# Sorting one batch's v in natural layout through DRAM, and a 96-column stationary operand for late scores, in a fused block-sort attention and feed-forward kernel

## The chip, the cores and the metric

The kernel runs on one core of a Trainium2 chip. The metric is device microseconds of one execution, the median of several. Most executions of the kernel before agree within 0.3%.

## The reference

Four batches of eight heads, 768 tokens, 64 values per head. A small matrix per head, made doubly stochastic by five rounds of normalisation (Sinkhorn), mixes ("sorts") the 8 blocks of 96 tokens of k and v. Each block of q then attends to its own sorted block, and the result goes through a feed-forward layer with a squared ReLU.

```python
k_sorted = np.einsum('bhij,bhjcd->bhicd', P, k_b)      # P: 8 x 8 per head, blocks of 96 tokens
v_sorted = np.einsum('bhij,bhjcd->bhicd', P, v_b)
scores = scale * np.matmul(q_b, k_sb.transpose(0, 1, 2, 4, 3))
attn = np.exp(scores - max); attn = attn / attn.sum()
x = np.matmul(attn, v_sb)                              # then (3072, 512) tokens
out = np.maximum(x @ w_in, 0.0) ** 2 @ w_out           # d_ff = 2048
```

## The kernel before

In a matmul call `lhsT` is the stationary operand, which a weight load puts into the array, and `rhs` is the moving one. A small planner orders all instructions ahead of time, so that attention work of the next batch stands between the feed-forward matmuls of the one before. Batches are numbered from 0 in the code and from one in the text. Heads are worked on in pairs (`hp`), in two groups (`g`) of two pairs.

The first two batches sort k and v with a product that transposes at the same time; v has to be turned back for the attention-value product:

```python
def s_sort(u, t, ...):                 # t: 1 = k, 2 = v
    for a in range(NA):                # 6
        for h in range(2):
            nc.tensor.matmul(out=tp[64 * h:64 * (h + 1), a, :],
                lhsT=src[:, 2 * u.hp + h, D * a:D * (a + 1)],          # 64 columns
                rhs=w_all[:, H * u.b + 2 * u.hp + h, ...])
def s_vt(u, ...):                      # 8 transposes of 128 x 128 turn v back
    nc.tensor.transpose(out=vbp[:, n, :], in_=u.vsT[:, i // NQ, ...], identity=ident)
```

The last two batches sort in natural layout with the array cut into 32x32 tiles. v is then written to DRAM and read back in another partition order, k is turned by a DMA transpose into `kx`. In `kx` the 8 blocks are interleaved, so one block's stationary operand is every eighth element:

```python
def s_nat(b, g, t, due):               # 16 matmuls of 32 x 32 weights, 384 columns
    ...
    nc.sync.dma_start(out=v_way[b, g]..., in_=vn_r[m]...)   # write
    nc.sync.dma_start(out=vb_r[w]..., in_=v_way[b, g]...)   # read back
def s_sc(u, ...):
    nc.tensor.matmul(out=scp[:, h, BLK * n:BLK * (n + 1)],
        lhsT=(u.ksT[64 * h:64 * (h + 1), hf, BLK * n:BLK * n + 128] if u.b < 2 else
              kx_r[u.kx][64 * h:64 * (h + 1), NQ * hf + n::NB]),    # 128 columns, step NB = 8
        rhs=...)                                                     # 96 columns
```

`kx` is 1024 elements wide, of which 256 are zeros, so that the operand has 128 columns although a block has only 96 tokens. Loads go through GpSimd's software DMA queue in a fixed order; two buffers each of q, k and v alternate between the batches.

The softmax here doesn't subtract the row's maximum and nothing guards it: scores larger than these inputs give would overflow.

Of the kernel before, what the change touches and what calls it, by code (L numbers as in the profile page):

```python
# [128 lines left out]
def kernel(  # L129
# [103 lines left out]
    for n in range(3):  # L233
        vb_r.append(const.tile([96, NB, HP, 66], BF16, name=f"vblk{n}"))
    v_way = nc.dram_tensor("v_way", (B, 2, NA, 128, HP * 66), BF16, kind="Internal").ap()

    kn_r = [const.tile([128, NA, 2, D], BF16, name=f"kn{n}") for n in range(3)]
    qi_r = [const.tile([128, NA, 2, D], BF16, name=f"qi{n}") for n in range(2)]
    kx_r = []
    for n in range(3):  # L240
        kx = const.tile([128, 128 * NB], BF16, name=f"kx{n}")
        nc.vector.memset(kx[:, 128 * NA:], 0.0)
        kx_r.append(kx)
    for n in range(4):
        et = const.tile([96, 2, HS + 32], BF16, name=f"et{n}")
        nc.vector.memset(et[:, :, HS:HS + 32], 0.0)
# [5 lines left out]
    xT = const.tile([128, KC, n_tok], BF16)  # L252
    w_all = const.tile([128, NH // 2, NB, C0], BF16)
    w_t = const.tile([128, NH // 4, 4, NB], BF16)
    qkv = {}
    landed = {}

# [14 lines left out]
    def load(b, t, h0, n, p=slice(0, 128)):  # L272
        def dst_src():
            alloc_qkv(b)
            if b > 1 and t:
                return (qkv[b][t].rearrange("p (g h) x -> p g (h x)", h=HP)[:, h0 // HP, :],
                        kv_t[t][b, :, h0 // HP, :])
            return qkv[b][t][p, h0:h0 + n, :], (q_r, k_r, v_r)[t][b, p, h0:h0 + n, :]
        dma((b, t, h0, p.start), 1.57 * n / H * (p.stop - p.start) / 128, dst_src,
            readers[b - 2] + [x_done[b - 1, x, 0] for x in range(HP)] if b > 1 else [])  # L280
# [26 lines left out]
    load_w_in(0)  # L307
    for g in range(1, 4):
        load_w_in(g)
    for g in range(4):  # L310
        t = slice(NT // 4 * g, NT // 4 * (g + 1))
        dma(("w_out", g), 1.05, lambda t=t: (w_out_bf[:, t, :], w_out_r[:, t, :]))
    for g in range(2):
        for t in (2, 1, 0):
            load(1, t, HP * g, HP)


    rs = const.tile([NH, NB], FP32)
# [83 lines left out]
    def build_wt(due):  # L402

        st = {}
        pick = const.tile([128, NB, 4], BF16, name="pick")
        picked = plan.add("DVE", 0.2, lambda e: nc.vector.tensor_copy(
            out=pick, in_=ident.rearrange("p (j c) -> p j c", c=C0)[:, :, 0:4]), [x_done[0, HP - 1, 0]])

        def mm(e):
            st["p"] = ps1.tile([128, NB, NH // 4], FP32, tag="p1", name="wtp")  # L410
            for h in range(4):
                nc.tensor.matmul(
                    out=st["p"][32 * h:32 * (h + 1), :, :].rearrange("p i g -> p (i g)"),
                    lhsT=pick.rearrange("p j c -> p (j c)"),
                    rhs=pt.rearrange("p i (g h) -> p h i g", h=4)[:, h, :, :],
                    start=True, stop=True)

        def fn(e):
            nc.vector.tensor_tensor(
                out=w_t,  # L420
                in0=mask_t[:, None, :, None].to_broadcast([128, NH // 4, 4, NB]),
                in1=st["p"].rearrange("p i g -> p g i")[:, :, None, :]
                .to_broadcast([128, NH // 4, 4, NB]),
                op=ALU.mult)

        s1, old = r1.take()
        pe = plan.add("PE", 0.15, mm, [cp, picked] + old, due, mode="col32")
        built["t"] = plan.add("DVE", 0.45, fn, [pe])
        r1.use(s1, pe, built["t"])


    class Unit:
# [101 lines left out]
    def s_sc(u, due=0):  # L534
# [3 lines left out]
        for hf in u.halves:  # L538
# [4 lines left out]
            def mm(e, hf=hf, st=st, slot=slot):  # L543
                qT = tiles["qT", u.b, u.hp]
                if u.b < 2:
                    qT = qT.rearrange("p a x -> p (a x)").rearrange("p (i q) -> p i q", q=BLK)
                st["p"] = scp = p2[slot]
                for n in range(NQ):
                    for h in range(2):
                        nc.tensor.matmul(  # L550
                            out=scp[:, h, BLK * n:BLK * (n + 1)],
                            lhsT=(u.ksT[64 * h:64 * (h + 1), hf, BLK * n:BLK * n + 128]
                                  if u.b < 2 else
                                  kx_r[u.kx][64 * h:64 * (h + 1), NQ * hf + n::NB]),
                            rhs=(qT[64 * h:64 * (h + 1), NQ * hf + n, :] if u.b < 2 else
                                 qT[64 * h:64 * (h + 1), :, C0 * (NQ * hf + n):
                                    C0 * (NQ * hf + n + 1)]),
                            start=True, stop=True)

            s2 = slot  # L560
            u.et[hf], olde = ret.take()
            pe = plan.add("PE", 0.17 if u.b < 2 else 0.26, mm, [u.k_op, u.q_op] + old, due,
                          mode="row")
            r2.use(s2, pe)
            rqT.use(qTs[u.b, u.hp], pe)
# [51 lines left out]
    def s_nat(b, g, t, due):  # L617
# [4 lines left out]
        for hp in (2 * g, 2 * g + 1):  # L622
            slot, old = r2.take()
            if t == 1:
                m, oldm = rkn.take()

            def mm(e, hp=hp, slot=slot):
                src = qkv[b][t].rearrange("p (g h) x -> p g (h x)", h=HP)
                for h in range(2):
                    r = slice(32 * (2 * (hp % 2) + h), 32 * (2 * (hp % 2) + h + 1))  # L630
                    for c in range(4):
                        nc.tensor.matmul(  # L632
                            out=p2[slot][32 * c:32 * (c + 1), h, 0:NA * D],
                            lhsT=w_t[r, HP // 2 * b + g, :, :].rearrange("p c i -> p (c i)"),
                            rhs=src[r, g, NA * D * c:NA * D * (c + 1)],
                            start=True, stop=True, tile_position=(r.start, 32 * c))

            def ev(e, hp=hp, slot=slot, m=m):
                dst = (vn_r[m][:, :, 2 * (hp % 2):2 * (hp % 2) + 2, 0:D] if t == 2
                       else kn_r[m])  # L640
                copy(e, dst, p2[slot][:, :, 0:NA * D].rearrange("p e (a d) -> p a e d", d=D))

            pe = plan.add("PE", 0.15, mm, [landed[b, t, HP * g, 0], built["t"]] + old, due,
                          mode="tile")
            readers[b].append(pe)
            op = plan.add(AD, cost_f(2 * NA * D), ev, [pe] + oldm)
            r2.use(slot, pe, op)
            evs.append(op)
            if t == 1:
                rkn.use(m, op)  # L650
                k_nat[b, hp] = m, op
# [1 line left out]
            return  # L653

        def write(e):
            nc.sync.dma_start(out=v_way[b, g].rearrange("a p x -> p a x"),
                              in_=vn_r[m].rearrange("p a h x -> p a (h x)"))

        w, oldw = rvb.take()

        def read(e):
            nc.sync.dma_start(
                out=vb_r[w].rearrange("p i h x -> p (i h x)"),
                in_=v_way[b, g].rearrange("a (c i) x -> (a c) (i x)", i=NB))

        wr = plan.add("SP", 0.33, write, evs + [loaded(b)])
        there = plan.add("WAY", 2.0, lambda e: None, [wr])
        rd = plan.add("SP", 0.33, read, [there] + oldw)
        back = plan.add("WAY", 2.0, lambda e: None, [rd])
        rvn.use(m, *evs, there)  # L670
        rvb.use(w, back)
        v_blk[b, g] = w, back
# [4 lines left out]
    def s_turn(b, hp):  # L677
# [3 lines left out]

        def k_turn(e):
            nc.sync.dma_start_transpose(
                out=kx_r[kx][:, 0:128 * NA].rearrange("p (a x) -> p a x", a=NA),
                in_=kn_r[m].rearrange("p a e d -> p (a e d)"))

        sp = plan.add("SP", 1.25, k_turn, [op, loaded(b)] + oldx)
# [26 lines left out]

    def s_av(u, due=0):
        nao, olda = rao.take()
        if u.b > 1:
            w, u.vs_op = v_blk[u.b, u.hp // 2]
        u.norms = []
        for hf in u.halves:  # L720
# [4 lines left out]
            def mm(e, hf=hf, st=st, slot=slot):  # L725
# [3 lines left out]
                for n in range(NQ):  # L729
                    for h in range(2):  # L730
                        nc.tensor.matmul(  # L731
                            out=oup[:, h, 66 * n:66 * n + D + 1],
                            lhsT=et_r[u.et[hf]][:, h, BLK * n:BLK * n + 128],
                            rhs=(u.vs[:, NQ * hf + n, h, 0:D + 1] if u.b < 2 else
                                 vb_r[w][:, NQ * hf + n, 2 * (u.hp % 2) + h, 0:D + 1]),
                            start=True, stop=True)

# [13 lines left out]
            op = plan.add("DVE", 0.9, norm, [pe])  # L751
            r2.use(s2, pe, op)
            ret.use(u.et[hf], pe)
            if u.b < 2:
                rks.use(u.n, pe)
            else:
                rvb.use(w, pe)
# [179 lines left out]
    def lay(b, halves, c0, c1):  # L937
        step, gap = (c1 - c0) / (HP + 0.9), (c1 - c0 - 13) / (HP - 1)
        for hp in range(HP):
# [3 lines left out]
            def open_(due, b=b, hp=hp, box=box):  # L943
# [2 lines left out]
                if b == 1:  # L946
                    build_w(H * b + 2 * hp, 2, pt, kops[b - 1, hp])
                u.k_op = kops[b, hp] = s_sort(u, 1, due)
                u.v_op = s_sort(u, 2, due)

            for f, s in ((0.0, open_),
                         (0.35, lambda due, box=box: s_sc(box["u"], due)),
                         (0.5, lambda due, box=box: s_vt(box["u"], due)),
                         (0.75, lambda due, box=box: s_av(box["u"], due)),
                         (1.2, lambda due, box=box: s_xt(box["u"], due))):
                todo.append((c + step * f, len(todo), s, b))
# [1 line left out]
    def lay_late(b, c0):  # L958

        todo.append((c0, len(todo), lambda due: load_late(b), 0))  # L960
        if b == 2:
            todo.append((c0, len(todo), build_wt, 0))
        for g in range(2):
            for t in (1, 2):
                todo.append((c0 + 9 + 9 * g, len(todo),
# [17 lines left out]
                load(b, t, HP * g, HP)  # L983

    lay(0, (1,), 0, n_up)
    lay(1, (0, 1), n_up, 2 * n_up)
    lay_late(2, 2 * n_up)
    lay_late(3, 4 * n_up)
# [45 lines left out]
```

## Time and profile before

| | before |
|---|---|
| median | 226.36 us (226.29 to 226.46, 4 runs) |
| span of the profiled run | 224.3 us |
| TensorE busy | 216.6 us, 97% |
| granted clock | 1.00 |

TensorE bounds the kernel; the prediction below shows the page's lines.

### The profile page before, as it was taken

How to read it: one execution, taken by the hardware profiler on the slowest of the kernel's cores; microseconds unless marked ns; L12 is line 12 of the kernel's file. 1: busy time of each engine (PE TensorE's matmuls, PEld its weight loads, DVE VectorE, ACT ScalarE, POOL GpSimd, SP SyncE). 2: the span in 40 equal slices, each digit the busy share in tenths (PEclk: the TensorE clock that was granted, in tenths of full speed). 3: DMA queues.
4: the chain of work that ended last, by engine and by line, in shares of the span. 5: the costliest groups of instructions: out<-in, count | busy, mean ns of one | idle time of the engine just before them, and what ended most of it. 6: DMA issues, size and time to landing. Idle time of an engine off the chain costs nothing.

```text
span 224.3 us, 5245 instructions
## 1 busy us (share of the span) xinstructions
PE 216.6 (97%) x2130; PEld 122.9 (55%) x2145; DVE 105.7 (47%) x297; ACT 122.1 (54%) x253; POOL 26.4 (12%) x46
## 2 busy tenths in 40 slices
PE   7898999999999999999999999999999999999994
PEld 2476665556665645545665455445665465446553
DVE  6777777317666416640666127523664045005400
ACT  4665776228885328734775248535774177137521
POOL 7962332200004200000000000000000000000000
PEclk9999999999999999999999999999999999999999
DMA  5999999999953996499941320899522410110012
GB/s 66 201 202 208 207 206 205 203 227 245 210 65 27 191 239 145 115 216 201 220 38 35 85 94 0 164 225 254 110 37 43 122 47 1 50 57 37 0 50 94
DMA packets 42744, 28.83 MB, mean 129 GB/s; under 512 B 22752, under 2 KB 38368, under 8 KB 42720
## 3 DMA queue, kind: packets, MB, share of 16 engines
q0 software_dynamic: 13888, 13.63, 37.1%
q1 hardware_dynamic: 28832, 14.86, 29.7%
q8 instruction: 17, 0.28, 0.5%
q14 instruction: 7, 0.06, 0.1%
HBM read 28.89 MB, written 7.91 MB: 164 GB/s over the span
## 4 chain that ended last, share of the span: by engine, by line
PE 92%; DMA 2%; DVE 2%; ACT 1%; issue 1%; ACTq 0%; POOLq 0%
PE hp L810 37%; PE op L838 35%; PE p L550 4%; PE p L731 3%; DMA qb<-in_q_dram 2%; PE p L510 2%; PE qtp L461 2%; PE vbp L598 2%; PE op L872 2%; PE p L350 1%; PE p L632 1%; PE xtp L779 1%; PE tp L510 1%; DVE ao L742 1%; ACT h L818 0%
## 5 line engine op out<-in xcount | busy, mean ns | idle before, releaser
L810 PE MATMUL hp<-xT,w_in_bf 128*128 128x384 bf16 x512 | 91.0, 326 | 0.0
L838 PE MATMUL op<-w_out_bf,h 128*128 128x512 bf16 x353 | 82.6, 379 | 0.8
L818 ACT ACTIVATE h<-hp 128x384 bf16<-128x384 f32 x128 | 62.0, 495 | 23.5 <-PE hp L810 20.0
L821 DVE TENSOR_TENSOR h<-h 128x384 bf16<-128x384 bf16 x128 | 44.5, 355 | 56.3 <-ACT h L818 55.5
L810 PEld LDWEIGHTS <-w_in_bf 128*128 128x128 bf16 x512 | 47.0, 98 | 30.0 <-issue 0.7
L838 PEld LDWEIGHTS <-h 128*128 128x128 bf16 x368 | 34.7, 98 | 39.4 <-issue 0.7
L192 ACT COPY ob<-op 128x512 f32<-128x512 f32 (+1 forms) x25 | 14.2, 569 | 56.0 <-PE op L838 50.6
L742 DVE TENSOR_TENSOR ao<-p,rec 96x512 bf16<-96x512 f32 x32 | 22.0, 687 | 1.4 <-DVE rec L741 0.3
L582 ACT ACTIVATE et<-p 96x384 bf16<-96x384 f32 x48 | 19.4, 491 | 2.4 <-PE p L550 2.4
L741 DVE RECIPROCAL rec<-p 96x8 f32<-96x8 f32 x32 | 6.4, 199 | 13.6 <-PE p L731 13.3
L731 PEld LDWEIGHTS <-et 96*128 96x128 bf16 x256 | 10.6, 97 | 2.9
L261 POOL DMA_DIRECT2D qb<-in_q_dram x8 | 6.0, 754 | 32.5 <-PE qtp L461 24.4
L350 PE MATMUL p<-ones 128*128 128x512 bf16 (+1 forms) x36 | 8.8, 360 | 1.1 <-DVE ones L213 1.1
L194 DVE COPY vs<-vbp 96x512 bf16<-96x512 bf16 (+1 forms) x12 | 6.1, 508 | 7.1 <-PE vbp L598 6.9
L573 ACT ACTIVATE et<-p 96x768 bf16<-96x768 f32 x8 | 6.3, 802 | 2.1 <-PE p L550 2.0
L261 POOL DMA_DIRECT2D kb<-in_k_dram x10 | 6.6, 659 | 6.6 <-DMA w_in_bf<-in_moe_w_in_dram 2.2
L261 POOL DMA_DIRECT2D vb<-in_v_dram x10 | 6.6, 660 | 6.4 <-DMA w_in_bf<-in_moe_w_in_dram 3.6
L192 ACT CAST ksT<-p 128x768 bf16<-128x768 f32 (+1 forms) x7 | 4.6, 662 | 3.3 <-PE p L510 3.3
L550 PEld LDWEIGHTS <-kx 64*128 64x128 bf16 x128 | 4.6, 155 | 2.8 <-issue 2.8
L731 PE MATMUL p<-vs,et 96*128 96x65 bf16 x128 | 6.0, 193 | 0.0
L461 PE MATMUL qtp<-ident,qb 64*64 64x64 bf16 (+1 forms) x144 | 4.7, 204 | 1.3 <-DMA qb<-in_q_dram 1.3
L461 PEld LDWEIGHTS <-qb 64*64 64x64 bf16 (+1 forms) x144 | 3.5, 109 | 4.5 <-DMA qb<-in_q_dram 2.3
(78 smaller groups left out, 129.3 us busy)
## 6 DMA issues: line engine op xcount, KB each, us to landing
out_dram<-ob SPq DMA_DIRECT2D x23, 256.0 KB, 2.8
qb<-in_q_dram POOLq DMA_DIRECT2D x8, 384.0 KB, 15.7
vb<-in_v_dram POOLq DMA_DIRECT2D x6, 384.0 KB, 17.1
kb<-in_k_dram POOLq DMA_DIRECT2D x6, 384.0 KB, 17.1
w_in_bf<-in_moe_w_in_dram POOLq DMA_DIRECT2D x4, 512.0 KB, 12.5
w_out_bf<-in_moe_w_out_dram POOLq DMA_DIRECT2D x4, 512.0 KB, 18.0
v_way<-vn SPq DMA_DIRECT2D x4, 396.0 KB, 4.1
vblk<-v_way SPq DMA_DIRECT2D x4, 396.0 KB, 3.9
```

The lines of the kernel that those rows point to most:

```text
L192: nc.scalar.copy(out=out, in_=in_)
L261: nc.gpsimd.dma_start(out=dst, in_=src)
L350: nc.tensor.matmul(out=out, lhsT=ones, rhs=rhs, start=True, stop=True)
L461: nc.tensor.transpose(out=t["p"][64 * h:64 * (h + 1), a, :], in_=qb[p0:p1, 2 * hp + h, D * a:D * (a + 1)], identity=ident[p0:p1, p0:p1])
L550: nc.tensor.matmul(out=scp[:, h, BLK * n:BLK * (n + 1)], lhsT=(u.ksT[64 * h:64 * (h + 1), hf, BLK * n:BLK * n + 128] if u.b < 2 else kx_r[ ...
L582: nc.scalar.activation(out=et[:, h, 0:HS].rearrange("p (n c a) -> p n c a", c=C0, a=NA), in_=st["p"][0:96, h, 0:HS].rearrange("p (n a c) - ...
L731: nc.tensor.matmul(out=oup[:, h, 66 * n:66 * n + D + 1], lhsT=et_r[u.et[hf]][:, h, BLK * n:BLK * n + 128], rhs=(u.vs[:, NQ * hf + n, h, 0: ...
L742: nc.vector.tensor_tensor(out=u.ao[:, n0:n0 + NQ, :, :].rearrange("p n e d -> p e n d"), in0=ov[:, :, :, 0:D], in1=rec[:, :, :, None].to_b ...
L810: nc.tensor.matmul(out=t["hp", nt][:, 0:HS], lhsT=w_in_bf[:, kc, 128 * nt:128 * (nt + 1)], rhs=xT[:, kc, t0:t0 + HS], start=(kc == 0), sto ...
L818: nc.scalar.activation(out=t["h1", nt], in_=t["hp", nt][:, 0:HS], func=AF.Relu)
L821: nc.vector.tensor_tensor(out=t["h2"][:, nt, :], in0=t["h1", nt], in1=t["h1", nt], op=ALU.mult)
L838: nc.tensor.matmul(out=t["op", mt], lhsT=t["h2"][:, nt, 128 * mt:128 * (mt + 1)], rhs=w_out_bf[:, nt, :], start=(nt == 0), stop=(nt == NT ...
```

## The change

Two intents. In the second batch, v takes the natural way that the late batches take (fewer and shorter matmuls, no turning back), with the DRAM round trip hidden beside the loads. And the late scores load only the 96 columns that a block has, instead of 128 with zeros.

```diff
-        kx = const.tile([128, 128 * NB], BF16, name=f"kx{n}")
-        nc.vector.memset(kx[:, 128 * NA:], 0.0)
-        kx_r.append(kx)
+        kx_r.append(const.tile([128, 128 * NA], BF16, name=f"kx{n}"))
...
+    load(1, 2, 0, HP)                      # first half of batch two's v, now ahead of w_out
     for g in range(4):
         dma(("w_out", g), ...)
-    for g in range(2):
-        for t in (2, 1, 0):
-            load(1, t, HP * g, HP)
+    for t, g in ((2, 1), (1, 0), (0, 0), (1, 1), (0, 1)):
+        load(1, t, HP * g, HP)
...
-                            out=scp[:, h, BLK * n:BLK * (n + 1)],
+                            out=scp[0:128 if u.b < 2 else 96, h, BLK * n:BLK * (n + 1)],
...
         def write(e):
+            for c in range(4):             # b == 1
+                nc.sync.dma_start(
+                    out=v_nat[b, g].rearrange("i (y z a) x -> z (i y) (a x)", z=4, a=NA)[c],
+                    in_=vn_r[m][32 * c:32 * (c + 1)].rearrange("p a h x -> p (a h x)"))
         def read(e):
+            if b == 1:
+                nc.sync.dma_start(
+                    out=vb_r[w].rearrange("p i h x -> p i (h x)"),
+                    in_=v_nat[b, g].rearrange("i p x -> p i x"))
...
-                u.v_op = s_sort(u, 2, due)
+                if b == 0:
+                    u.v_op = s_sort(u, 2, due)
+            if b == 1 and hp % 2 == 0:
+                todo.append((14 + 6 * hp, len(todo),
+                             lambda due, g=hp // 2: s_nat(1, g, 2, due), b))
```

Cut: the weights for the new sort (`w_v`), their earlier construction, the branches that keep the late batches as they were, the later use of the read-back tile, and the bookkeeping of buffers. Comments are added.

More of the change, by code (lines that the diff above doesn't have):

```diff
@@ L235 @@
     v_way = nc.dram_tensor("v_way", (B, 2, NA, 128, HP * 66), BF16, kind="Internal").ap()
+    v_nat = nc.dram_tensor("v_nat", (B, 2, NB, BLK, HP * 66), BF16, kind="Internal").ap()
     kn_r = [const.tile([128, NA, 2, D], BF16, name=f"kn{n}") for n in range(3)]
@@ L254 @@
     w_t = const.tile([128, NH // 4, 4, NB], BF16)
+    w_v = const.tile([128, 2, NB, 4], BF16)
     qkv = {}
@@ L274, in dst_src @@
             alloc_qkv(b)
-            if b > 1 and t:
+            if b > 1 and t or b == 1 and t == 2:
                 return (qkv[b][t].rearrange("p (g h) x -> p g (h x)", h=HP)[:, h0 // HP, :],
@@ L424, in fn, with fn1 @@
                 op=ALU.mult)
+        def fn1(e):
+            nc.vector.tensor_tensor(
+                out=w_v,
+                in0=mask_t[:, None, None, :].to_broadcast([128, 2, NB, 4]),
+                in1=st["p"][:, :, 2:4].rearrange("p i g -> p g i")[:, :, :, None]
+                .to_broadcast([128, 2, NB, 4]),
+                op=ALU.mult)
         s1, old = r1.take()
         pe = plan.add("PE", 0.15, mm, [cp, picked] + old, due, mode="col32")
+        built["v"] = plan.add("DVE", 0.25, fn1, [pe])
         built["t"] = plan.add("DVE", 0.45, fn, [pe])
-        r1.use(s1, pe, built["t"])
+        r1.use(s1, pe, built["v"], built["t"])
     class Unit:
@@ L561, in s_sc @@
             u.et[hf], olde = ret.take()
-            pe = plan.add("PE", 0.17 if u.b < 2 else 0.26, mm, [u.k_op, u.q_op] + old, due,
+            pe = plan.add("PE", 0.17 if u.b < 2 else 0.21, mm, [u.k_op, u.q_op] + old, due,
                           mode="row")
@@ L628, in mm @@
                 src = qkv[b][t].rearrange("p (g h) x -> p g (h x)", h=HP)
+                w = (w_v[:, g, :, :].rearrange("p i c -> p (i c)") if b == 1 else
+                     w_t[:, HP // 2 * b + g, :, :].rearrange("p c i -> p (c i)"))
                 for h in range(2):
@@ L633, in mm @@
                             out=p2[slot][32 * c:32 * (c + 1), h, 0:NA * D],
-                            lhsT=w_t[r, HP // 2 * b + g, :, :].rearrange("p c i -> p (c i)"),
+                            lhsT=w[r, :],
                             rhs=src[r, g, NA * D * c:NA * D * (c + 1)],
@@ L655, in write @@
         def write(e):
-            nc.sync.dma_start(out=v_way[b, g].rearrange("a p x -> p a x"),
-                              in_=vn_r[m].rearrange("p a h x -> p a (h x)"))
+            if b > 1:
+                nc.sync.dma_start(out=v_way[b, g].rearrange("a p x -> p a x"),
+                                  in_=vn_r[m].rearrange("p a h x -> p a (h x)"))
+                return
+            for c in range(4):
+                nc.sync.dma_start(
+                    out=v_nat[b, g].rearrange("i (y z a) x -> z (i y) (a x)", z=4, a=NA)[c],
+                    in_=vn_r[m][32 * c:32 * (c + 1)].rearrange("p a h x -> p (a h x)"))
         w, oldw = rvb.take()
         def read(e):
+            if b == 1:
+                nc.sync.dma_start(
+                    out=vb_r[w].rearrange("p i h x -> p i (h x)"),
+                    in_=v_nat[b, g].rearrange("i p x -> p i x"))
+                return
             nc.sync.dma_start(
@@ L664, in read @@
                 in_=v_way[b, g].rearrange("a (c i) x -> (a c) (i x)", i=NB))
-        wr = plan.add("SP", 0.33, write, evs + [loaded(b)])
-        there = plan.add("WAY", 2.0, lambda e: None, [wr])
+        wr = plan.add("SP", 0.33, write, evs + ([loaded(b)] if b > 1 else []))
+        slow = 6.0 if b == 1 else 2.0
+        there = plan.add("WAY", slow, lambda e: None, [wr])
         rd = plan.add("SP", 0.33, read, [there] + oldw)
-        back = plan.add("WAY", 2.0, lambda e: None, [rd])
+        back = plan.add("WAY", slow, lambda e: None, [rd])
         rvn.use(m, *evs, there)
@@ L683, in k_turn @@
             nc.sync.dma_start_transpose(
-                out=kx_r[kx][:, 0:128 * NA].rearrange("p (a x) -> p a x", a=NA),
+                out=kx_r[kx].rearrange("p (a x) -> p a x", a=NA),
                 in_=kn_r[m].rearrange("p a e d -> p (a e d)"))
@@ L716, in s_av @@
         nao, olda = rao.take()
-        if u.b > 1:
+        if u.b > 0:
             w, u.vs_op = v_blk[u.b, u.hp // 2]
@@ L733, in mm @@
                             lhsT=et_r[u.et[hf]][:, h, BLK * n:BLK * n + 128],
-                            rhs=(u.vs[:, NQ * hf + n, h, 0:D + 1] if u.b < 2 else
+                            rhs=(u.vs[:, NQ * hf + n, h, 0:D + 1] if u.b < 1 else
                                  vb_r[w][:, NQ * hf + n, 2 * (u.hp % 2) + h, 0:D + 1]),
@@ L753, in s_av @@
             ret.use(u.et[hf], pe)
-            if u.b < 2:
+            if u.b < 1:
                 rks.use(u.n, pe)
@@ L948, in open_ @@
                 u.k_op = kops[b, hp] = s_sort(u, 1, due)
-                u.v_op = s_sort(u, 2, due)
+                if b == 0:
[3 more added lines that the diff above has]
+                             lambda due, g=hp // 2: s_nat(1, g, 2, due), b))
             for f, s in ((0.0, open_),
                          (0.35, lambda due, box=box: s_sc(box["u"], due)),
-                         (0.5, lambda due, box=box: s_vt(box["u"], due)),
+                         (0.5, lambda due, box=box: b == 0 and s_vt(box["u"], due)),
                          (0.75, lambda due, box=box: s_av(box["u"], due)),
@@ L960, in lay_late @@
         todo.append((c0, len(todo), lambda due: load_late(b), 0))
-        if b == 2:
-            todo.append((c0, len(todo), build_wt, 0))
         for g in range(2):
@@ L985 @@
     lay(0, (1,), 0, n_up)
+    todo.append((8, len(todo), build_wt, 0))
     lay(1, (0, 1), n_up, 2 * n_up)
```

## The prediction

> **What bounds the kernel now.** I read the page's busy table first, then the chain that ended last, then the same chain in order of time for single stretches, then the waits and the DMA issues.
>
> ```profile
> PE 216.6 (97%) x2130; PEld 122.9 (55%) x2145; DVE 105.7 (47%) x297; ACT 122.1 (54%) x253; POOL 26.4 (12%) x46
> PE   7898999999999999999999999999999999999994
> DMA  5999999999953996499941320899522410110012
> PE 92%; DMA 2%; DVE 2%; ACT 1%; issue 1%; ACTq 0%; POOLq 0%
> ```
>
> TensorE is busy for 97% and carries 92% of the last chain; no other engine passes 55%. From 22 us to 179 us it idles under 1 us in all (stretches of 27.1, 47.6, 48.0 and 34.5 us show 26.9, 47.4, 47.8 and 34.3 busy). So a matmul group taken out of the stream there shortens the run by its own length, as long as its place in the stream is not filled by a wait. The DMA digits show the one thing that could do that: the queue is full from 6 us to about 56 us, just where the change adds transfers.
>
> The chain in order of time (start us, length us, what) is the price list. The second batch begins at 49.46; its heads come in four pairs, here the first two, then one natural sort and one late score group:
>
> ```profile
> 49.46 0.46 PE qtp L461 x12
> 49.91 0.67 PE p L510 x24
> 50.59 1.41 PE hp L810 x8
> 51.99 0.45 PE p L550 x16
> 52.44 0.55 PE vbp L598 x8
> 52.99 1.30 PE hp L810 x8
> ...
> 55.91 0.34 PE p L510 x12
> 56.25 0.76 PE hp L810 x4
> 57.00 0.46 PE p L510 x12
> 57.46 0.76 PE hp L810 x4
> 58.22 0.28 PE p L550 x8
> 58.49 0.02 issue
> 58.51 0.35 PE p L550 x8
> 58.86 0.76 PE hp L810 x4
> 59.62 0.45 PE vbp L598 x8
> ...
> 88.64 0.31 PE p L632 x16
> 88.95 1.41 PE hp L810 x8
> ...
> 102.85 0.63 PE p L550 x16
> ```
>
> L510 is the sort of k or v through the transposing product, L598 turns v back, L550 are the scores, L632 is the natural-layout sort, and L810 is feed-forward filler. Eight hp take 1.30 after a group in the same array mode and 1.41 after one in another; four take 0.65 or 0.76. So leaving a tiled mode costs 0.11 us, charged to the group behind it.
>
> [...] the strided kx: its sixteen score matmuls run as 8 pairs (one per row half) 62 ns apart, read from single starts, while the packed ksT, also 128 wide, runs pairs 40 ns apart. The 64-column loads of L510, [...] give 31.6 ns per pair with 64 moving columns. 62/128 and 31.6/64 are both 0.49 ns a column, so kx already loads at the plain rate and there is nothing to lose. [...] The trace's 0.49 ns a column decides: 47 ns, above the 40 ns that 96 moving columns take. [...] loads of 384 KB land 1.9 to 2.0 us apart, but 3.0 us apart (45.33 to 48.36) around an output store of 256 KB.
>
> **Part by part.** All at the full clock (PEclk is 9 in every slice).
> *Removed: the v sorts of batch two.* Pair one: half of the x24 group, 0.34. Pairs two and three: own groups of 0.46 plus 0.11 for leaving the mode, 0.57 each. Pair four has an x24 of 0.80 where k alone takes 0.34: 0.46. Sum 1.94.
> *Removed: the turns back.* 0.45 each when they follow filler; the 0.55 behind scores contains their 0.11, which filler will pay instead. 4 x 0.45 = 1.80.
> *Removed: a wait.* In pairs two and three the scores take 0.64 (58.22 to 58.86) against 0.45, since both PSUM buffers are still being emptied of k and v. With v gone k has one of them long before: 2 x 0.19 = 0.38.
> *Added: two natural sorts of v.* x16 each, 0.31 plus 0.11 = 0.42, so 0.84. (A 0.53 elsewhere in the chain has a down-projection record missing, 0.22 us.)
> *Added: one split.* In the new instruction order pair four's q turn and k sort are no longer neighbours but have filler between: one more entry and exit, 0.23.
> *Moved.* The small product for the natural weights goes from 82 us to about 35 us at the same cost. v comes from the read-back tile in the attention-value product; 128 such matmuls of the late batches average 193 ns, the same as with the old tile: nothing.
> *Late scores.* 8 groups, each 8 pairs of 47 instead of 62 ns: 8 x 0.12 = 0.96.
> Net: -1.94 - 1.80 - 0.38 + 0.84 + 0.23 - 0.96 = -4.0 us, so 222.3 if no new wait shows.
> ScalarE and VectorE lose four evictions of v (768 columns) and four of its turn, and gain four of 768 columns; both stay near half busy. The three dropped memsets lie at the start, beside the first loads: nothing.
>
> **The transfers.** Loads are issued in order and land in order. One v load (2.0 us) now goes ahead of w_out, whose four parts landed at 29.9, 32.5, 35.1 and 37.6. They move to about 31.9 to 39.6. The first write to DRAM of 396 KB, cut in four, should go out near 37 us and take some 1.5 us of the queue (from 1.05 us for a 256 KB store), so the last part lands at 40 to 41. The chain has its first use near 41.3; the inserted 0.67 us makes that about 41.9. Margin about 1 us. The q of batch two's first half landed at 43.4 and was needed at 49.46. Ahead of it stand now one more load (2.0), the write (1.5) and perhaps the read back (1.5): 48.5, against a need near 50.5. The read back itself: write out near 37, landing after 5 to 6 us as stores did there (5.3 to 6.5 against 2.0 on an idle queue), read the same again: about 49, needed near 54. The second half's: about 60, needed near 66. Every item fits, two of them narrowly.
>
> **Rivals.** (a) *A late w_out or q becomes the wait.* For it: the DMA digits of 9 until 56 us and margins of 1 to 2 us built from estimates. Against: the weights' other parts have slack, and a stall lets the queue catch up. It would cost 0.5 to 2 us: 222.8 to 224.3. (b) *The 96-column load is slower or no faster.* [...] If just unchanged: 223.3. Against: the common 0.49 ns. (c) *The read back is late for the attention-value product,* [...] For it: each read waits on SyncE for its write. Against: 5 us of slack, three output buffers. It would cost 1 to 3 us. (d) *PSUM.* The natural sorts use the two attention buffers in the first batch's phase, 0.9 us an eviction: some tenths.
>
> **Range and chances.** From 222.3 I add 0.4 for rivals (a) and (d), about half of their likely size: 222.7, 1.6% less. For over 2% it has to come below 221.9: all of the sum and some unseen wait besides, 0.17. Slower by 2% (over 230.9) needs a broken transfer path: 0.01. The low end is the sum plus 0.6 us of luck; the high end has rival (a) in full or (b) at no gain.
>
> **What would show it.** Right: no v in the transposing sort in 49 to 97 us, 32 fewer turns, late score groups of about 0.51 us in the chain, their loads' pairs 47 ns apart, TensorE idle under 1.5 us between 22 and 180 us. Wrong: a TensorE or weight-load wait on the DMA of w_out near 41 us, of q near 50 us or of the read back near 54 or 66 us; late score pairs 62 ns or more apart; attention waits on VectorE or ScalarE where the natural sorts stand near 35 and 47 us.

## More of the kernel before

One more row matters later: the loads of the late scores' stationary operand, from the groups of weight loads by form (columns: line, engine, operation, operand, rows*columns and elements, count | busy us, mean ns of one | idle time before, what ended it).

```profile
L550 PEld LDWEIGHTS <-kx 64*128 64x128 bf16 x128 | 4.6, 155 | 2.8 <-issue 2.8
```

155 ns for a 128-column load, where the packed `ksT` of the early batches, of the same 64x128 form, takes 94 and the packed weights of the feed-forward layer 98: the step of 8 elements is not free.

## The result, and the profile after

The changed kernel takes **238.69 us** (238.21 to 239.38, 4 runs), against 226.36. The ratio is 1.0547, with a 95% interval of 1.0521 to 1.0573: slower by 5.5%, where 222.7 us had been predicted. A ratio here is the mean time of one kernel's runs over that of the other's of the same rounds, so it is not quite the ratio of the medians. Executions over 1.5% slower than the fastest of the same kernel are left out of the means.

The page of the changed kernel: busy engines, TensorE's digits (40 slices of 5.9 us), the granted clock, and the chain that ended last by engine and by line.

```profile
PE 223.3 (95%) x2082; PEld 128.3 (54%) x2097; DVE 103.3 (44%) x291; ACT 122.9 (52%) x253; POOL 25.9 (11%) x46
PE   6998999999928999999999999999999999999994
PEclk9999999999986999999999999999999999999999
PE 81%; DMA 8%; DVE 5%; ACT 2%; issue 2%; POOL 1%; SPq 1%; POOLq 0%; ACTq 0%
PE op L862 33%; PE hp L834 31%; PE p L559 6%; DMA vblk<-v_nat 5%; DMA v_nat<-vn 3%; PE p L755 3%; PE p L644 2%; PE op L896 1%; DVE ao L766 1%; PE vbp L607 1%; PE p L519 1%; PE xtp L803 1%; PE tp L519 1%; DVE p_sb L330 1%; SPq L673 1%
```

TensorE has fewer instructions and is busy 6.7 us longer. There is a hole at slice 12, near 68 us, with a lower clock around it, and transfers hold 8% of the chain. Both sides of the loss show in the chain in order of time (start us, us, what):

```profile
49.05 0.42 PE p L644 x16
...
51.82 7.07 DMA v_nat<-vn
...
59.03 12.22 DMA vblk<-v_nat
71.25 0.14 issue
71.39 1.04 PE p L755 x16
...
73.21 1.39 PE hp L834 x4
...
107.44 1.54 PE p L559 x16
```

The second natural sort of v (L644) ends at 49.5, its last piece is written by 58.9, and the read back takes 12.2 us. The attention-value product (L755) of the third pair could have started near 66.3 us (TensorE has done all before it by then) and starts at 71.4. Behind the hole the same four filler matmuls take 1.39 us where they took 0.76. Then the late scores: a group of sixteen takes 1.54 us, where the same group took 0.63. The load group by form says it is the load:

```profile
L559 PEld LDWEIGHTS <-kx 64*96 64x96 bf16 x128 | 11.9, 267 | 2.7 <-issue 2.4 <-DMA vblk<-v_way 0.3
```

A load of 96 columns takes 267 ns, one of 128 took 155.

The busy times by stretch show the hole and the low clock (stretch, its length, then busy us of PE, PEld, DVE, ACT and POOL with counts, granted clock, DMA share, GB/s):

```profile
66.00:71.40 5.40, 0.46 (x4) 0.10 (x3) 0.00 (x0) 1.69 (x5) 0.00 (x0) 0.74 1.11 214
71.40:76.00 4.60, 4.38 (x41) 2.65 (x44) 2.85 (x8) 1.29 (x2) 1.49 (x2) 0.57 0.40 49
```

During the hole the 16 DMA engines are busy throughout (share 1.11, 214 GB/s), so the transfer that TensorE waits for shares them with something. What, the timeline of GpSimd's issues tells. Before (start us, us, engine and line, operation, tiles, count, idle time and what ended it):

```profile
70.57 0.75 POOL L261 DMA_DIRECT2D qb<-in_q_dram  x1 [24.43 <-PE qtp L461]
```

This was the first load of batch four; all six waited for q's buffer. After:

```profile
49.76 0.53 POOL L261 DMA_DIRECT2D vb<-in_v_dram  x1 [3.15 <-PE p L644]
51.32 0.53 POOL L261 DMA_DIRECT2D vb<-in_v_dram  x1 [1.04 <-DMA qb<-in_q_dram]
73.51 0.75 POOL L261 DMA_DIRECT2D qb<-in_q_dram  x1 [21.66 <-PE qtp L470]
```

The natural sort (L644) is done with batch two's v some 20 us earlier than the transposing sort was. So batch four's two v loads are issued at 50 us into a queue that is still full: it now empties near 71 us instead of 63.

### The profile page after: what moved, and what is told of

Its sections match the earlier page's. It is cut to its first block, busy times and chain, and to the rows that moved or that the text cites. A ratio compares the mean times of both kernels' runs of the same rounds, so it can differ in the third digit from the quotient of the medians.

```text
span 236.1 us, 5159 instructions
## 1 busy us (share of the span) xinstructions
PE 223.3 (95%) x2082; PEld 128.3 (54%) x2097; DVE 103.3 (44%) x291; ACT 122.9 (52%) x253; POOL 25.9 (11%) x46
## 4 chain that ended last, share of the span: by engine, by line
PE 81%; DMA 8%; DVE 5%; ACT 2%; issue 2%; POOL 1%; SPq 1%; POOLq 0%; ACTq 0%
PE op L862 33%; PE hp L834 31%; PE p L559 6%; DMA vblk<-v_nat 5%; DMA v_nat<-vn 3%; PE p L755 3%; PE p L644 2%; PE op L896 1%; DVE ao L766 1%; PE vbp L607 1%; PE p L519 1%; PE xtp L803 1%; PE tp L519 1%; DVE p_sb L330 1%; SPq L673 1%
## 5 line engine op out<-in xcount | busy, mean ns | idle before, releaser
L845 DVE TENSOR_TENSOR h<-h 128x384 bf16<-128x384 bf16 x128 | 44.2, 355 | 64.4 <-ACT h L842 63.4
L192 ACT COPY ob<-op 128x512 f32<-128x512 f32 (+1 forms) x24 | 13.6, 567 | 56.1 <-PE op L862 50.6
L755 PEld LDWEIGHTS <-et 96*128 96x128 bf16 x256 | 10.9, 99 | 8.1 <-issue 5.3
L559 PEld LDWEIGHTS <-kx 64*96 64x96 bf16 x128 | 11.9, 267 | 2.7 <-issue 2.4
L755 PE MATMUL p<-vblk,et 96*128 96x65 bf16 x192 | 8.5, 197 | 4.9 <-DMA vblk<-v_nat 4.9
L559 PE MATMUL p<-qT,kx 64*96 64x96 bf16 x128 | 12.9, 341 | 0.0
L192 ACT COPY qT<-qtp 128x384 bf16<-128x384 bf16 (+1 forms) x11 | 5.6, 553 | 5.9 <-PE qtp L470 5.9
L194 DVE CAST vn<-p 128x768 bf16<-128x768 f32 x6 | 5.7, 958 | 3.8 <-PE p L644 3.7
L261 POOL DMA_DIRECT2D vb<-in_v_dram x10 | 6.1, 613 | 10.0 <-PE p L644 3.2
```

The lines of the kernel that those rows point to most:

```text
L192: nc.scalar.copy(out=out, in_=in_)
L261: nc.gpsimd.dma_start(out=dst, in_=src)
L559: nc.tensor.matmul(out=scp[0:128 if u.b < 2 else 96, h, BLK * n:BLK * (n + 1)], lhsT=(u.ksT[64 * h:64 * (h + 1), hf, BLK * n:BLK * n + 128 ...
L755: nc.tensor.matmul(out=oup[:, h, 66 * n:66 * n + D + 1], lhsT=et_r[u.et[hf]][:, h, BLK * n:BLK * n + 128], rhs=(u.vs[:, NQ * hf + n, h, 0: ...
L845: nc.vector.tensor_tensor(out=t["h2"][:, nt, :], in0=t["h1", nt], in1=t["h1", nt], op=ALU.mult)
```

## The experiments

"Inserted" below means the start of the next feed-forward matmul less the start of the last one before a group, less the latter's own time in an unbroken stream (0.16 us for `hp`, 0.22 for `op`). It includes entering and leaving an array mode, and is read from single starts in the trace.

### late128: the changed kernel with 128 columns again

```diff
-        kx_r.append(const.tile([128, 128 * NA], BF16, name=f"kx{n}"))
+        kx = const.tile([128, 128 * NB], BF16, name=f"kx{n}")
+        nc.vector.memset(kx[:, 128 * NA:], 0.0)
+        kx_r.append(kx)
```

Cut: the matching widths of the score output and of k's transpose, and the planner's guess of a group's time; the same goes for only96.

> The changed kernel with the late scores' stationary operand back at 128 columns (and its zeroed tail); the v path stays. Theory: the 96-column load costs 0.91 us in each of the 8 late score groups (1.64 against 0.73 us inserted into the stream), so this run should gain 7.3 us on the changed kernel and land near 231.4 us, with score groups of 0.73 us again and the stall of some 5 us before the third attention-value product of batch two still there. Rival: the late groups are slow because of something that the v path does to the machine (a lower clock after the stall, traffic); then they stay above 1.2 us here and the time stays above 235.

Measured: 231.56 us (230.99 to 232.0), 1.022 of before (1.0199 to 1.0241). Score groups cost 0.72 us inserted again, and the stall is there: the read back is issued at 60.0 and lands at 71.3. What follows: the columns cost 7.1 us, apart from the rest. What is left is a loss of 2.2% against the kernel before, clear of noise.

### only96: the kernel before with 96 columns alone

```diff
-                            out=scp[:, h, BLK * n:BLK * (n + 1)],
+                            out=scp[0:128 if u.b < 2 else 96, h, BLK * n:BLK * (n + 1)],
```

with the narrower `kx`, as in the change.

> The kernel before with one edit: the late scores' stationary operand has 96 columns, no zeroed tail. Theory: 8 groups x 0.91 us, so 226.4 + 7.3 = 233.7 us, no new wait elsewhere. Rival as for the run with 128 columns: the loss needs the v path; then this run stays within 1 us of 226.4, or gains the 1 us that was predicted.

Measured: 233.69 us (233.58 to 233.83), ratio 1.0321, granted clock 1.0. All eight groups cost 1.64 us inserted, against 0.72. The loss needs nothing of the v path.

### stridemap and colmap: what a load costs, by columns and step

The late scores of the kernel before, each of the eight head pairs with its own column count and step (results wrong; cut: `MAP`, the table of counts and steps, and the score output cut to the same count):

```diff
-                                  kx_r[u.kx][64 * h:64 * (h + 1), NQ * hf + n::NB]),
+                                  kx_r[u.kx][64 * h:64 * (h + 1), NQ * hf + n:NQ * hf + n
+                                        + MAP[u.b, u.hp][1] * (MAP[u.b, u.hp][0] - 1) + 1:MAP[u.b, u.hp][1]]),
```

> The kernel before, wrong results on purpose: each of the 8 late head pairs reads its stationary operand with another column count and step between columns: 128 columns at steps 8, 4, 2, 1, then 96 columns at steps 8, 4, 2, 1. Theory A (below 128 columns the load leaves a fast path, and the slow path is what suffers from the step): 128 columns cost 62 ns a pair at step 8 and about 40 at step 1, and 96 columns about 176 ns a pair at step 8 but at most 60 at step 1. Theory B (96 columns are slow by themselves, whatever the step): 96 columns stay near 176 ns a pair at step 1 too. Theory C (step 8 alone costs, in proportion to the columns): 96 at step 8 would be cheaper than 128 at step 8, which the changed kernel already speaks against.

> As the map of steps, wrong on purpose: column counts 127, 120, 112 and 80 at step 8, then 127, 112 and 80 at step 1 and 96 at step 3. If exactly 128 columns are what makes a fast load, 127 at step 8 is the slowest of all (176 x 127/96 = 233 ns a pair) and the cost falls with the count: 120 near 220, 112 near 205, 80 near 147. If instead only counts that leave a quarter of the array idle are slow, 127, 120 and 112 stay near 62 ns. At step 1 the counts should cost about 0.49 ns a column or the 40 ns of the moving columns, whichever is more: 62, 55 and 40 ns; 96 at step 3 lies between 47 and 176.

The chain in order of time of the map of steps: 128 columns at steps 8, 4, 2, 1, then 96 columns at steps 8, 4, 2, 1.

```profile
102.84 0.63 PE p L553 x16
108.62 0.46 PE p L553 x16
113.59 0.45 PE p L553 x16
118.54 0.45 PE p L553 x16
...
150.67 1.54 PE p L553 x16
157.35 0.86 PE p L553 x16
162.72 0.51 PE p L553 x16
167.74 0.49 PE p L553 x16
```

The same view of the map of counts, here 127 and 80 columns at step 8, and 127 at step 1:

```profile
102.85 1.99 PE p L553 x16
...
122.68 1.30 PE p L553 x16
...
155.66 0.60 PE p L553 x16
```

Taking away one column of 128 makes the group three times as long (0.63 to 1.99). Per pair of loads (one for each row half), from single starts:

| columns | step 1 | step 2 | step 3 | step 4 | step 8 |
|---|---|---|---|---|---|
| 128 | 42 | 42 | | 42 | 62 |
| 127 | 58 | | | | 233 |
| 120 | | | | | 220 |
| 112 | 52 | | | | 207 |
| 96 | 46 | 47 | 69 | 91 | 176 |
| 80 | 42 | | | | 147 |

(ns; no entry falls below 42, and the packed `ksT` gives 40, which is 0.42 ns for each of the 96 moving columns, as in `hp`, with 384 in 0.16 us.) From 80 to 127 columns the cost at step 8 is proportional to the columns, 1.83 to 1.85 ns a column; at steps 1 and 2 it is 0.46 to 0.49 ns a column from 96 columns on, and 96 columns give 0.72 and 0.95 at steps 3 and 4. From step 2 on that is about 0.23 ns times the step (0.23 to 0.25). With 128 columns, a quarter of that law gives 0.23 x 8 x 128 / 4 = 59 ns, and 62 was measured. So theory A holds: of the counts tried (80, 96, 112, 120, 127 and 128) only 128 loads fast, about four times as fast where the step makes the load visible (62 against 233 ns for 127), and the step of 8 slows both ways of loading (128 columns: 62 against 42 ns; 96 columns: 176 against 46). Theories B and C fall, and so does the idea that only some counts below 128 are slow. It is width and step together that cost: 96 columns at step 1 or 2 take 46 or 47 ns a pair, less than the 62 of the kernel before, and 128 columns at steps 1 to 4 take 42. So a smaller step, not fewer columns, is what the late scores could gain from; no kernel with such a layout of `kx` was run.

### hold3: the two early v loads of batch four wait for the read back

A tiny GpSimd copy, from the read-back tile into the buffer that the load will fill, makes each load wait:

```diff
+            if gate is not None:
+                nc.gpsimd.tensor_copy(out=dst[0:32, 0:2], in_=vb_r[gate][0:32, 0, 0, 0:2])
             nc.gpsimd.dma_start(out=dst, in_=src)
...
+        held = b == 3 and t == 2
```

(shortened to the case of a two-dimensional destination; this and all runs below have 128 columns)

> The 128-column version of the changed kernel (231.6 us), and the two v loads of batch four, which it issues at 50 us because the natural sort frees their buffer early, made to wait for the second read back by a tiny GpSimd copy of a read-back element into each buffer. Theory 1 (these two extra loads prolong the full queue, and the small packets of the read back only get through when it empties): the queue empties near 66.5 instead of 71 us, the read back lands near 67 instead of 71.3 us, the stall falls from 5.5 to about 1 us, the low clock after it mostly goes: 226 to 227 us. Theory 2 (the read is slow by itself, 528-byte pieces written shortly before): it still takes 11 to 12 us and the time stays near 231.

Measured: 227.47 us (226.23 to 229.29; the two longest executions have a mean granted clock of 0.99), 1.0044 of before (0.9985 to 1.0102). In the profiled execution, the shortest of the four, the last load lands at 66.8 and the read back at 68.2; the group with the attention-value product costs 3.06 us inserted, against 6.46 in the 128-column version and 1.12 without a stall; the clock is 1.0. Theory 1, with a wider spread than expected and a read 1.4 us behind the last load.

### holdall: all loads of batches three and four wait

```diff
-        held = b == 3 and t == 2
+        held = b >= 2
```

The edit is shown against hold3.

> As the previous run, but all loads of batches three and four wait for the second read back, so the queue is empty from about 51 us on. Theory 1 (contention): the write takes about 3.5 us, the read 4 to 5 us as the other re-tiling reads do (landing near 59 us, needed at 66.5); no stall; TensorE idles under 1 us between 22 and 180 us; full clock; 224 to 225 us, 2 us below the kernel before. The loads of batch three then land by 75 us and are needed at 88 us. Theory 2 (slow by itself): the read takes over 9 us, landing at 64 or later.

Measured: 228.39 us, the median of three executions (226.43 to 228.46; a fourth, of 230.69, was slow), 1.005 of before, where 224 to 225 had been expected. The queue empties at 51.9; the read, issued at 54.3, takes 3.75 us, and the stall at 66 us is gone. The read is not slow by itself. But the time is no better than before, because a new wait stands at 81 us:

```profile
68.70 15.03 DMA xT<-ao
...
83.77 6.23 PE hp L841 x27
```

This is its chain in order of time: the held loads now run until 93 us, and the transposed output of batch two, issued at 68.7, takes 15 us among them. TensorE waits 2.8 us for it, and then runs at a granted clock of 0.5 from 84.5 to 87.9 us. So holding everything moves the wait.

### early, and early_hold3: the second natural sort six filler groups earlier

```diff
-                todo.append((14 + 6 * hp, len(todo),
+                todo.append((14 + 3 * hp, len(todo),
```

> The 128-column version with the second natural sort of v placed 6 filler groups earlier (near 43 instead of 49 us; its input landed at 40.9 us); no load is held. Theory 1, in its strong form (the read back can't finish before the load queue empties near 71 us): the read is issued 4 to 6 us earlier and still lands at 67 to 71 us; stall 1 to 5 us, 227 to 231 us. Rival (the sort simply stands too late, and a read takes 9.5 to 11 us beside loads wherever it stands): it lands near 63 us, no stall, about 224.5 us.

> Both: the second natural sort 6 groups earlier and the v loads of batch four held until the read back. Theory 1: the queue empties near 66.5 us and the read, issued near 53 us, lands between 63 and 67 us: stall under 1 us, 224.3 to 225.5 us. Rival as for the earlier sort alone: lands near 63 us, about 224.5 us, so this run and the earlier sort alone would come out equal.

Measured: 231.95 us (231.38 to 232.62) for the earlier sort alone, and 226.5 us (225.8 to 228.88) with the two v loads held as well, where 224.3 to 225.5 had been expected: there the read landed at 67.7, just past the expected 67, and TensorE still waited 1.2 us for it. Alone, the read is issued at 56.1, 4 us earlier than in the 128-column version, takes 15.8 us, and lands at 71.9. Its wait, from the list of waits:

```profile
PE p L757 <- DMA vblk<-v_nat: 5.2, 1, 5.2
```

An earlier start bought nothing, which is what the strong form of theory 1 asked for, and the rival (the sort simply stands too late) falls: the two runs differ by 5.4 us.

### smallrows: the competing loads with small packets

The k and v loads of batch three go back to the layout of the early batches, so that they write packets of 768 bytes instead of 3072 (batch three's result is wrong).

```diff
-            if b > 1 and t or b == 1 and t == 2:
+            if b == 3 and t or b == 1 and t == 2:
```

> The 128-column version of the changed kernel, with the k and v loads of batch three taken in the layout of the early batches, so that they write 768-byte packets instead of 3072-byte ones (batch three's result is wrong on purpose; the two v loads of batch four keep 3072). Theory 1a (engines take turns packet by packet, so a read of 528-byte packets gets a share that falls with the size of the other queue's packets): the second read back, issued near 60 us, gets through in 8 to 10 us, landing near 69 us while the last loads (near 71 us or later) are still out: 2 us or more before the last landing. Theory 1b (whatever the packets, this read lands when the queue empties): it lands within 0.5 us of the last load again, 11 to 12 us after its issue.

Measured: the read, issued at 57.3, lands at 66.0, after 8.7 us, and 10.5 us ahead of the last load (76.4). That is theory 1a: beside 768-byte packets the read took 8.7 us, beside 3072-byte packets, in late128, 11.2.

The packet records of the traces show how the read and the loads shared the engines. In both runs 3.5 us pass from the issue to the read's first packet (60.8 us here, 62.5 in the changed kernel; in the empty queue of holdall it is 1.0 us). From there on the DMA engines moved about one packet of the read for each packet of the loads, at the same total rate: 682 beside 655 of 768 bytes here (61 to 65 us, 216 GB/s), 325 beside 292 of 3072 bytes in the changed kernel (63 to 68 us, 217 GB/s), 461 beside 411 in early (61 to 68 us). That is 170 packets of 528 bytes a microsecond here and 65 in the changed kernel. An estimate from these rates for all 768 packets is 4.5 us here and 11.8 us there, if the loads last; from first to last packet the traces show 4.7 us here, 11.5 in early, and 8.3 in the changed kernel, whose loads thin out from 68.5 us on. The size of the read's own packets was not varied.

The time, 234.49 us, is no gain: the queue stays full longer, and the transposed outputs of batch two, with 256-byte packets, now take 18 to 21 us, so that the feed-forward waits for one:

```profile
PE hp L836 <- DMA xT<-ao: 6.6, 1, 6.6
```

### holdmix and holdmix2: clear the queue twice

In the first, the second-half k and v loads of batch three wait for the read back, and all loads of batch four wait for the third transposed output of batch two. In the second, the first-half k and v loads of batch three are held as well.

```diff
+        if b == 2 and h0 and t:            # holdmix2: if b == 2 and t
+            gate = lambda: vb_r[v_blk[1, 1][0]][0:32, 0, 0, 0:2]
+        if b == 3:
+            gate = lambda: xT[0:32, 2, S:S + 2]
```

Cut: the dependencies that tell the planner the same.

> The 128-column version of the changed kernel with the queue kept clear twice: the second-half k and v loads of batch three wait for the second read back of v, and all loads of batch four wait for the third transposed output of batch two. Theory 1 (reads and transposes with small packets land when the load queue empties): the queue empties near 62.7 us, the read back (issued near 59 us) lands near 64 us, before its need at 66.2 us; the transposed outputs of batch two land within 6 us of their issue; no TensorE wait on a transfer between 30 and 180 us; full clock; 224.3 to 225 us, 0.7 to 1% below the kernel before, with a narrow spread again. Rival (some other wait of the v path shows up as the stall goes, as it did when all loads were held): above 226 us.

> As the previous run, but the first-half k and v loads of batch three are held as well, so the queue empties near 59 us: the read back should take under 5 us and land near 63 us. If the previous run already has no stall, this one equals it (224.3 to 225 us); if its margin of 2 us is too small in some executions, this one has the narrower spread. If holding more loads starves the transposed outputs of batch two instead, as in the run that held everything, a wait of 1 to 3 us comes back near 80 us.

Measured: **224.09 us** (223.82 to 224.46, 4 runs) for the first, 0.9895 of before (0.9882 to 0.9908); its result is correct, and it beats both kernels (by 1.05% and 6.1%). Its page:

```profile
PE 215.5 (97%) x2097; PEld 120.2 (54%) x2097; DVE 103.7 (47%) x294; ACT 121.8 (55%) x253; POOL 27.2 (12%) x54
PE 93%; DMA 2%; DVE 2%; issue 1%; ACT 1%; ACTq 0%; POOLq 0%
```

TensorE is at 97% again, and transfers are back to 2% of the chain. The second takes 225.72 us (224.81 to 227.26, 6 runs), 0.9974 of before, more than the 224.3 to 225 expected: no stall near 66 us either, but the fourth natural sort of batch three costs 2.0 us inserted, against 0.63. There a transpose of k, issued at 90.1, lands at 95.3, against 94.0 in the first, beside loads that now run until 91.8. That this transpose is the cause was not tested.

The second read back in all these runs, by the times of issue and landing in the traces (us):

| run | read issued | last load of the full stretch lands | read lands | took |
|---|---|---|---|---|
| changed kernel | 59.0 | 70.9 | 71.3 | 12.2 |
| late128 | 60.0 | 71.0 | 71.3 | 11.2 |
| early | 56.1 | 71.6 | 71.9 | 15.8 |
| early_hold3 | 56.0 | 67.3 | 67.7 | 11.8 |
| hold3 | 59.1 | 66.8 | 68.2 | 9.2 |
| holdmix | 58.5 | 63.2 | 64.4 | 5.9 |
| holdmix2 | 57.3 | 58.8 | 61.2 | 3.9 |
| holdall | 54.3 | 51.9 | 58.0 | 3.75 |
| smallrows | 57.3 | 76.4 | 66.0 | 8.7 |

## Why the prediction was wrong, point by point

Two steps of the prediction failed: that 96 columns have "nothing to lose", and that the second read back lands at about 60 us. Differences of runs split the loss. The columns cost 7.1 us (changed kernel less late128). The stall and its aftermath cost 7.5 us (late128 less holdmix). The v path with the loads held gains 2.4 us (before less holdmix). These must add up to the measured 12.3 whatever the causes are, since they lead step by step from one kernel to the other; the sum is no check. The checks are others: only96 less before gives 7.2 us for the columns without any v path, and late128's trace shows 5.3 us more in the stalled group than holdmix's (6.46 against 1.12 inserted) and 1.2 us in slower filler behind it, 6.5 of the 7.5. The kernel before with its loads held was not run; as it idles under 1 us between 22 and 179 us, holding has little to gain there.

- **What bounds the kernel** held: TensorE, and groups taken out of its stream are gained in full. Batch two's heads went from 11.87 us inserted (less 0.22 for a filler record that is missing in the trace) to 8.15 in holdmix, 3.7 us less; the sum of 1.94 + 1.80 + 0.38 - 0.23 had said 3.9. The small wait before the scores of pairs two and three is gone, as foretold: 0.54 inserted instead of 0.74.
- **"There is nothing to lose"** in going from 128 to 96 columns failed, and it was worth 8 us: -0.96 predicted, +7.2 measured. The step was "62/128 and 31.6/64 are both 0.49 ns a column, so kx already loads at the plain rate". The two rates are equal by accident. The 64-column loads are packed and, at 0.49 ns a column, fit the slow law at step 1; the kx loads were on the fast path, about four times as fast (62 ns a pair for 128 columns, 233 for 127), and had a step of 8 that costs about four times as much (176 against 46 ns for 96 columns). I had measured neither fewer columns at step 8 nor another step, and put an inference from two different situations in their place. Rival (b) in the prediction named the direction, but the step's price was not in it.
- **"The second half's: about 60, needed near 66"** failed. The need was right (66.3). The landing was 71.3: the write went out some 2 us later than assumed, its last piece took 7.1 us, and the read took 12.2 us instead of the 5 to 6 that I took over from output stores in the same full queue. Stores have 2048-byte packets and the read back 528-byte ones; that difference was never looked at, nor the 3072-byte packets of the loads beside it. The first read back shows it as well: 9.4 us instead of "5 to 6", but with slack.
- **The full queue was misread, and taken from before** ("full from 6 us to about 56 us"). The ten 9s of the DMA digits reach from 5.6 to 61.7 us, and the last load before landed at 63.0, so the second round trip lay in a full queue from the start. The change moved its end further: freeing v's buffer early let 0.8 MB of batch four's loads in, and the round trips themselves added 1.6 MB. Nothing in the prediction asked what an earlier release would start.
- **Rival (c)** named this wait but put it down to SyncE, where each read waits for its write, and priced it at 1 to 3 us. The stall was 5 us, and it cost 7.5 in all, for the clock dropped: the 4.6 us after the hole ran at 0.57.
- **Natural sorts at 0.42 each**: a sort that stands alone costs that (0.41 in holdmix), but the sum was too low. The first batch's phase grew by 1.77 us, of which 0.25 is the moved small product: 1.5 for two sorts instead of 0.84. The rest lies in neighbours: a turn costs 0.15 us more behind the small product and 0.29 more behind the first sort, and a k and v sort costs 0.84 instead of 0.59. I did not test why.
- **Rival (a)** (late w_out or q) did not happen. The last w_out part landed at 39.0 and q at 45.8; TensorE waits for neither beyond the start.

What stays open: why 3.5 us pass before the read's first packet in a full queue and 1.0 us in an empty one, and whether larger packets in the read itself would have been enough.

## What to carry to other kernels

Before narrowing a stationary operand, check whether its width buys a fast load; here the zero columns that kept it at 128 were worth more than the columns saved, above all at step 8 (62 against 176 ns a pair for 128 and 96 columns; 42 against 46 at step 1). The read through the full queue was priced by its number of packets and by the size of the packets that alternated with them (65 packets a microsecond beside 3072-byte ones, 170 beside 768-byte ones), not by a transfer of similar size. And when a change frees a buffer earlier, look up which load that lets go, and whether something urgent stands behind it in the queue; here, with 128 columns kept, holding back eight loads turned a loss of 2.2% into a gain of 1.05%.

## What the runs measured of the chip

- Weight loads by columns: 128 against 127 columns at step 8 took 62 against 233 ns per pair of loads. By step: without the fast path the price is about 0.23 ns per column and element of step from step 2 on (96 columns: 47, 69, 91, 176 ns at steps 2, 3, 4, 8; 46 at step 1); with it, 128 columns take 42 ns at steps 1, 2 and 4 and 62 ns at step 8.
- Single loads against pairs: at 127 columns and step 1 a pair takes 58 ns in the stream, though a single load lasts 135 ns in the trace.
- Reads beside loads: the 396 KB read of 528-byte packets took 3.75 us in an empty queue (holdall), 8.7 beside 768-byte packets (smallrows) and 12.2 beside 3072-byte packets in the changed kernel (11.2 and 15.8 in late128 and early). The packets of the two queues passed in nearly equal numbers (325 beside 292 in the changed kernel, 682 beside 655 in smallrows). The transposed outputs, with 256-byte packets, have a median of 2.8 us in the changed kernel, and took 15 us in holdall and up to 21 in smallrows.
- The granted clock after a wait: in holdall, a wait of 2.8 us was followed by a granted clock of 0.5 from 84.5 to 87.9 us; in the changed kernel it was 0.5 from 68.6 to 75.4 us, from 2.1 us after TensorE fell idle at 66.4. After waits of 1.9 us (hold3) and 1.3 us (holdmix2) it stayed at 1.0 in the profiled executions.
